# Transposing the heads of the second chunk by DMA, and holding back half of two weight matrices, in an AdaLN transformer block

## The chip, the cores and the metric

The kernel runs on one core of a Trainium2 chip. The metric is the device time of one execution in microseconds (us). Every time below is of that core. One further execution was recorded by the hardware profiler; its span runs from the first to the last instruction that the profiler saw.

## What is computed

A transformer block with adaptive layer norm: a sequence of S = 2048 rows of D = 640 values in bf16, 32 heads of 20, causal attention with a window of 256 rows, and a gated MLP of width 1536. Cut to what matters:

```python
mod = (silu(c) @ w_mod).reshape(1, 6, 1, -1)
sa, ca, ga, sb, cb, gb = mod[:, 0], ..., mod[:, 5]

h = layernorm(x) * (1 + ca) + sa
q, k, v = heads(h @ wqkv)                        # 32 heads of 20
scores = einsum('bhqd,bhkd->bhqk', q, k) * 20 ** -0.5
scores = where(0 <= i - j < 256, scores, -1e9)
x = x + ga * (merge(softmax(scores) @ v) @ wo)

h = layernorm(x) * (1 + cb) + sb
x = x + gb * ((sigmoid(h @ w_gate) * (h @ w_up)) @ w_down)
```

## The kernel before, in words

**Tiles and stages.** `build` cuts the 2048 rows into eight chunks of 256 rows (`NCH`, `CH`), numbered `a` from 0, each of two blocks of 128 rows (`bi`). All weights stay in SBUF once loaded: `wqkv`, `wo`, `wg` (w_gate), `wu` (w_up), `wd` (w_down). The weights of the modulation are needed only at the start and are loaded in the space of others: the first part in that of `wd`, others in that of `wu` and of `hh`, the MLP's hidden values. So the loads of `wu` wait until the modulation rows that used its space are computed (`extra=o1`, line 1217).

For each chunk the stages are:

- `ln1(a)` (line 833): statistics on VectorE (DVE), normalised rows on GpSimd (POOL) or DVE, then the transposed `hT`. For the first three chunks it is turned on TensorE (PE) against an identity matrix, for the others by a transposing DMA (`transp_dma`, lines 780 to 783, on SyncE's queue, SP) and then modulated (`modulate`, L790 and L791).
- `qkv(a)` (line 868): projections through `wqkv`, in pieces of 320 columns for chunk 0 and of 480 for the others. `evac` (lines 856 to 863) copies each piece from PSUM to `stg`, on ScalarE (ACT, L859) or DVE (L860); V goes to its own tiles. In `stg` a head takes 32 columns. It has four slots, each with q or k of one block of 128 rows: 128 x 1024.
- **Turning the heads.** Scores need q and k with the head's 20 values on partitions: `QT` and `KT`. Line 903 decides how a `stg` slot is turned. For chunks `a < NPQ` PE does it, in two halves of four 128x128 transposes into one PSUM tile (L911, recorded at L666, the line of the helper `mm`), and `evac` copies 512 columns out. For later chunks one transposing DMA turns the slot as a whole (line 919, recorded at L782). With PE the two halves of a slot come free to their readers one by one; with the DMA both halves come together.
- `attention(a)` (line 1074): for each half `q` of the heads five score sets (four for the heads, one for the edges of the window); for chunk 0 three. `score_set` (line 931) writes scores into the single score buffer in PSUM (PE, L667), and the exponentials are taken from it by ACT (L981). POOL masks them (L1006). Then comes a burst of 64 matmuls with V (`burst`, line 1019), which runs within a later score set, and the normalisation on DVE (`norm`, line 1044). The rows go out to DRAM and come back as `oT`, by DMA. The first score set of a chunk reads `QT` of both blocks and `KT` of its own and the previous chunk.
- `outproj(a)` (line 1113) and `mlp(a)` (line 1161): output projection, second layer norm, `h2T` by transposing DMA; then gate and up for 128 columns of FF at a time, in pairs, their product into `hh`, and the product with `wd`. Pairs from the seventh on (`f0` of 6 or more) read the second half of the columns of `wg` and `wu`.

**Loads.** `load_bulk` (line 607) splits a weight matrix by tiles of 128 rows. `wg` and `wu` are each loaded in two halves of 768 columns, and each half as a piece of three row tiles (576 KB) and one of two (384 KB): line 744 for `wg`, line 1217 for `wu`. Most of the DMAs, the transposing ones among them, go out on SP's one queue, in program order; a DMA that waits for its source holds those behind it. Each DMA also waits for the one 24 places earlier (`NDMA`), whose semaphore it takes over.

**Order.** All operations are first collected by `Prog.op`, each with a rough duration, its reads and writes, a priority and at times an earliest time (`tmin`). `Prog.schedule` (line 152) uses these to give every tile its slot. The order that runs is written out by hand, or by a search: `PRIO` (lines 341 to 464) holds a number for each operation, in the order of their making. Sorted by these numbers, the operations stand in the order of the program on each engine; the remainder of such a number after division by 5 names its engine (PE, ACT, DVE, POOL, SP). At run time nothing but these queues and the semaphores counts: `tmin` holds nothing back by itself.

Of the kernel before, what the change touches and what calls it, by code (L numbers as in the profile page):

```python
# [336 lines left out]
def c_pe(n):  # L337
# [5 lines left out]
    13, 18, 68, 1113, 43, 33, 8, 23, 53, 58, 38, 63, 48, 372, 73, 3, 96, 104, 81, 189, 199, 194, 204, 209, 219, 249,  # L343
    214, 244, 239, 234, 414, 599, 874, 574, 899, 909, 1239, 884, 904, 135, 142, 171, 177, 182, 77, 110, 115, 120,
    125, 255, 260, 265, 28, 130, 270, 290, 275, 280, 285, 295, 300, 375, 305, 322, 604, 889, 879, 1574, 914, 894,
    107, 147, 157, 92, 87, 152, 163, 168, 222, 227, 315, 350, 310, 380, 385, 340, 326, 356, 332, 391, 347, 362, 367,
    337, 401, 396, 430, 435, 446, 655, 660, 677, 480, 486, 750, 756, 415, 420, 426, 490, 495, 501, 465, 471, 650,
    682, 450, 455, 461, 520, 525, 531, 505, 577, 625, 632, 475, 510, 516, 620, 640, 646, 665, 671, 965, 981, 720,
    725, 732, 850, 865, 946, 745, 760, 767, 770, 785, 791, 547, 537, 552, 542, 442, 557, 563, 568, 612, 637, 795,
    775, 735, 855, 700, 847, 782, 742, 862, 707, 960, 970, 976, 1090, 1100, 1202, 1030, 1077, 1355, 1362, 1165,  # L350
    1170, 1191, 1277, 1205, 1291, 1375, 1382, 990, 995, 1001, 1025, 1045, 1051, 1365, 1371, 1280, 1336, 1005, 1010,
    1016, 1021, 1095, 1177, 1240, 1246, 1180, 1185, 1196, 1265, 1270, 1297, 1310, 1317, 1479, 1644, 1322, 1437,
    2114, 1494, 1894, 1499, 1862, 1902, 1922, 1947, 2142, 1385, 1522, 1529, 2854, 1467, 1507, 254, 409, 607, 952,
    957, 932, 617, 987, 1058, 1063, 1068, 1143, 1107, 1455, 1415, 1420, 1400, 1300, 1462, 1432, 1426, 1412, 1307,
    1610, 1620, 1627, 1545, 1550, 1557, 1649, 1615, 1630, 1636, 1667, 1654, 1870, 1880, 1966, 2040, 2050, 2057,
    2334, 2030, 2035, 2047, 2137, 2119, 1785, 1795, 1912, 1975, 1980, 1987, 714, 719, 917, 922, 1072, 927, 937, 942,
    1118, 1123, 1128, 1133, 1222, 1139, 1234, 1608, 1598, 1593, 1473, 1536, 580, 586, 591, 685, 691, 696, 800, 816,
    826, 806, 836, 823, 833, 813, 843, 1080, 1212, 1147, 1217, 1227, 1287, 1821, 1841, 1541, 1351, 2006, 1035, 1041,
    1086, 1150, 1156, 1161, 1250, 1326, 1391, 1341, 1256, 1333, 1398, 1348, 1263, 1500, 1512, 1517, 1562, 1662,
    1672, 1836, 1801, 1846, 1856, 2011, 2200, 2270, 2302, 2150, 2160, 2307, 2145, 2155, 2282, 2410, 2415, 2422,  # L360
    2312, 2317, 2442, 2432, 2427, 2437, 2448, 2453, 2457, 2462, 2554, 2559, 2758, 2743, 2748, 2716, 2753, 2564,
    2829, 2964, 2859, 3037, 3047, 3387, 3042, 3052, 3342, 3352, 3362, 3368, 3347, 3357, 3477, 2885, 2890, 2895,
    2900, 2905, 2765, 2770, 2775, 2790, 2880, 2916, 2942, 3085, 3090, 3115, 3120, 3125, 2910, 3095, 3100, 3105,
    3110, 3131, 3137, 3140, 3145, 3150, 3175, 3180, 3205, 3210, 3215, 3220, 3225, 3186, 3237, 3240, 3245, 3250,
    3255, 3260, 3230, 3265, 3270, 3275, 3280, 3286, 3292, 3295, 3300, 3305, 3320, 3325, 3390, 3395, 3400, 3405,
    3410, 3331, 3442, 3445, 3450, 3455, 3460, 3465, 3415, 3420, 3470, 3530, 3565, 3486, 3592, 3515, 3670, 3720,
    3727, 3730, 3745, 3750, 3757, 4119, 3765, 3805, 3830, 3872, 3660, 3665, 3825, 3877, 3884, 1715, 1790, 1867,
    1875, 1955, 1972, 2104, 1720, 1725, 1806, 1812, 2109, 2390, 2395, 2402, 2285, 2290, 2296, 2409, 2250, 2320,
    2326, 2532, 2339, 1915, 1950, 2026, 1730, 1755, 1997, 1406, 1484, 1762, 1752, 1777, 1767, 1567, 1772, 1783,
    1898, 2088, 2183, 2078, 2128, 2189, 2174, 2363, 2371, 2386, 2376, 2381, 1440, 1451, 1446, 1575, 1581, 1586,  # L370
    1675, 1701, 1681, 1736, 1696, 1740, 1826, 1816, 1830, 1851, 1886, 1960, 2016, 2021, 1533, 1713, 1708, 1603,
    1688, 1693, 1908, 2068, 1928, 2063, 2073, 2083, 2090, 2096, 2211, 2207, 2197, 2277, 2597, 2602, 2874, 2869,
    2984, 2849, 2994, 2220, 2236, 2226, 2241, 2246, 2340, 2346, 2356, 2465, 2496, 2476, 2480, 2485, 2627, 2470,
    2490, 2506, 2714, 2615, 2620, 2657, 2672, 3029, 2520, 2525, 2587, 2535, 2540, 2611, 2639, 2680, 2685, 2812,
    2816, 3034, 2650, 2665, 2787, 2795, 2875, 2937, 1659, 1489, 1992, 1937, 2002, 1932, 1747, 1942, 2123, 2133,
    2168, 2193, 2693, 2698, 2549, 2709, 3542, 2921, 3506, 3426, 3431, 2500, 2516, 2511, 2178, 2263, 2268, 2218,
    2233, 2258, 2353, 2578, 2368, 2573, 2568, 2583, 2590, 2641, 2646, 2662, 2782, 2807, 2822, 2947, 2974, 2954,
    2959, 2969, 2989, 3495, 3500, 3547, 3520, 3525, 3572, 3555, 3560, 3677, 3580, 3585, 3682, 3597, 3692, 3697,
    3702, 3687, 3707, 3713, 3718, 3777, 3862, 3784, 3869, 4158, 4153, 4143, 4021, 4136, 4175, 4300, 4310, 4315,
    4320, 4160, 4210, 4305, 4330, 4335, 4326, 4347, 4340, 4435, 4440, 4445, 4450, 4390, 4395, 4425, 4430, 4460,  # L380
    4456, 4552, 4465, 4470, 4475, 4480, 4485, 4560, 4565, 4570, 4575, 4580, 4496, 4602, 4585, 4590, 4595, 4660,
    4665, 4605, 4610, 4670, 4675, 4685, 4681, 4692, 4695, 4700, 4705, 4710, 4715, 4725, 4730, 4735, 4745, 4750,
    4721, 4767, 4770, 4780, 4830, 4835, 4840, 4805, 4810, 4815, 4820, 4825, 4846, 4857, 4850, 4915, 4920, 4927,
    5150, 5250, 5260, 5322, 5326, 5065, 5070, 5075, 5107, 5330, 5335, 5340, 5347, 5529, 2675, 2726, 2731, 2736,
    2721, 2830, 2836, 2841, 3055, 3061, 3066, 3170, 3196, 3191, 2703, 3018, 2803, 2763, 3008, 2998, 3003, 3023,
    3013, 3078, 3073, 3083, 3310, 3316, 3336, 3372, 3382, 3437, 3552, 3842, 4064, 4059, 3849, 3854, 4069, 3480,
    3511, 3601, 3606, 3491, 3610, 3641, 3616, 3735, 3741, 3796, 3760, 3925, 3932, 4200, 4205, 4227, 4239, 4075,
    4085, 4102, 4107, 4234, 4110, 4180, 4187, 3915, 3920, 3936, 4424, 3945, 3950, 4017, 4082, 4419, 3965, 3970,
    4012, 4070, 4090, 4097, 2631, 2606, 3157, 3162, 3167, 2927, 2932, 3377, 3658, 3898, 3902, 3912, 3999, 4054,
    4993, 4546, 4557, 4966, 4266, 3810, 3821, 3816, 3203, 3623, 3638, 3628, 3788, 3633, 3653, 3648, 3773, 3793,  # L390
    3803, 3893, 3940, 3956, 3961, 4002, 4007, 4352, 4357, 4362, 4369, 4384, 4374, 4379, 4389, 4910, 4930, 4937,
    4940, 4945, 4952, 4985, 5005, 5027, 5010, 5015, 5032, 5022, 5082, 5087, 5057, 5037, 5062, 5093, 5098, 5157,
    5162, 5174, 5169, 5401, 5367, 5388, 5392, 5396, 5430, 5435, 5440, 5445, 5450, 5490, 5495, 5500, 5505, 5510,
    5481, 5522, 5515, 5540, 5545, 5550, 5555, 5535, 5565, 5575, 5580, 5585, 5561, 5592, 5745, 5750, 5755, 5760,
    5825, 5775, 5785, 5790, 5850, 5855, 5831, 5867, 5875, 5880, 5885, 5895, 5900, 5860, 5890, 5905, 5930, 5965,
    5911, 5987, 5970, 5975, 5980, 5990, 5995, 6000, 6005, 6010, 6015, 6055, 6021, 6062, 6085, 6090, 6095, 6100,
    6105, 6065, 6070, 6075, 6080, 6130, 6111, 6197, 6285, 6350, 6355, 6432, 6760, 6845, 6855, 6862, 6956, 6370,
    6655, 6745, 6802, 6850, 6915, 6945, 6952, 6964, 4025, 4046, 4036, 4031, 4041, 4120, 4131, 4126, 4260, 4271,
    4281, 4400, 4406, 4411, 4173, 4193, 4198, 4148, 4293, 4168, 4248, 4253, 4258, 4278, 4288, 4298, 4500, 4531,
    4526, 4512, 4507, 4517, 4742, 4862, 5229, 5179, 5234, 4869, 5239, 4615, 4626, 4621, 4631, 4636, 4775, 4786,  # L400
    4796, 4880, 4886, 4891, 6440, 6445, 6467, 6470, 6475, 6481, 6489, 6490, 6520, 6527, 6536, 6559, 6515, 6540,
    6547, 6415, 6420, 6426, 6554, 6580, 6585, 6596, 6601, 6609, 5110, 5120, 5266, 5360, 5420, 5427, 2864, 2979,
    3537, 3887, 3907, 3577, 3837, 3857, 3978, 3983, 3987, 3992, 4219, 4224, 4493, 4538, 4762, 4756, 4521, 4955,
    4971, 4976, 4653, 4648, 4658, 4543, 4643, 4878, 4793, 4873, 4803, 4898, 4908, 4903, 5040, 5046, 5051, 5102,
# [57 lines left out]
NPQ = 2  # L462
# [810 lines left out]
```

## Time and profile before

| | |
|---|---|
| median of three runs | 328.59 us (327.43, 328.59, 805.26) |
| profiled execution, its own time | 327.7 us |
| its span | 326.0 us |
| its mean granted clock of PE | 1.00 |
| busy: PE, DVE, ACT, POOL | 318.1, 208.2, 210.6, 187.4 us |
| instructions: PE, DVE, ACT, POOL | 4877, 416, 311, 282 |
| mean DMA rate over the span | 116 GB/s |

The profiled execution took 1.7 us more than its span. A busy time is the sum of an engine's instructions, without its waits, its branches and the issuing of DMAs. The page also divides the span into 40 slices, with the busy share of each engine in tenths; PEclk there is the clock that PE was granted. Groups of instructions stand as `line engine operation output<-input shapes xcount | busy us, mean ns of one | idle us of the engine just before them, and what ended most of it`. A line of the timeline begins with start and length in us. One of the chain of waits too: it is the work that ended last, followed back step by step to what released it. PE M stands for matmuls other than scores, PE S for scores.

### The profile page before, as it was taken

How to read it: one execution, taken by the hardware profiler on the slowest of the kernel's cores; microseconds unless marked ns; L12 is line 12 of the kernel's file. 1: busy time of each engine (PE TensorE's matmuls, PEld its weight loads, DVE VectorE, ACT ScalarE, POOL GpSimd, SP SyncE). 2: the span in 40 equal slices, each digit the busy share in tenths (PEclk: the TensorE clock that was granted, in tenths of full speed). 3: DMA queues.
4: the chain of work that ended last, by engine and by line, in shares of the span. 5: the costliest groups of instructions: out<-in, count | busy, mean ns of one | idle time of the engine just before them, and what ended most of it. 6: DMA issues, size and time to landing. Idle time of an engine off the chain costs nothing.

```text
span 326.0 us, 11617 instructions
## 1 busy us (share of the span) xinstructions
PE 318.1 (98%) x4877; PEld 223.6 (69%) x4878; DVE 208.2 (64%) x416; ACT 210.6 (65%) x311; POOL 187.4 (57%) x282
## 2 busy tenths in 40 slices
PE   8999999979999999999999999999999999999996
PEld 3664644536876568765777567877786788787885
DVE  4598998559897847776576456846383666363332
ACT  1698985797875788858687878785778671021120
POOL 6119588989829795737483859564848493013000
PEclk9999999999999999999999999999999999999999
DMA  7989898999850535405804582510132131302101
GB/s 242 369 274 364 222 243 210 194 136 217 243 114 0 115 95 100 95 4 137 128 23 54 120 132 69 117 39 4 62 58 68 42 70 35 102 22 43 40 2 40
DMA packets 71694, 37.85 MB, mean 116 GB/s; under 512 B 45274, under 2 KB 70362, under 8 KB 71642
## 3 DMA queue, kind: packets, MB, share of 16 engines
q1 hardware_dynamic: 68800, 34.82, 44.6%
q10 hardware_dynamic: 2842, 2.30, 2.7%
q8 instruction: 38, 0.62, 0.8%
q14 instruction: 14, 0.11, 0.1%
HBM read 21.30 MB, written 5.25 MB: 81 GB/s over the span
## 4 chain that ended last, share of the span: by engine, by line
PE 80%; DMA 1%; ACT 1%; DVE 0%; issue 0%
PE M L666 66%; PE S L667 7%; PE M L667 6%; DMA QT<-stg 1%; ACT E L981 1%; DVE stg L860 0%; ACT V L859 0%; DVE x L1196 0%; DVE x L1130 0%
## 5 line engine op out<-in xcount | busy, mean ns | idle before, releaser
L981 ACT ACTIVATE E<-S 128x512 bf16<-128x512 f32 (+2 forms) x184 | 150.8, 879 | 49.5 <-PE S L667 46.9
L1006 POOL TENSOR_SCALAR_AFFINE_SELECT E<-E 128x512 bf16<-128x512 bf16 (+1 forms) x176 | 141.1, 830 | 68.0 <-ACT E L981 65.5
L666 PE MATMUL M<-wqkv,hT 128*128 128x480 bf16 (+1 forms) x340 | 73.4, 355 | 1.1 <-ACT hT L790 0.5
L666 PE MATMUL M<-h2T,wg 128*128 128x256 bf16 x480 | 66.1, 273 | 0.0
L666 PE MATMUL M<-h2T,wu 128*128 128x256 bf16 x480 | 66.0, 273 | 0.0
L666 PE MATMUL M<-wd,hh 128*128 128x320 bf16 (+1 forms) x396 | 59.0, 295 | 0.0
L1175 ACT ACTIVATE sig<-M 128x512 f32<-128x512 f32 x48 | 28.6, 602 | 44.0 <-PE M L666 33.8
L1177 DVE SCALAR_TENSOR_TENSOR hh<-sig,M 128x512 bf16<-128x512 f32 x48 | 32.3, 676 | 37.0 <-PE M L666 17.8
L666 PEld LDWEIGHTS M<-h2T,wu 128*128 128x128 bf16 x480 | 45.6, 98 | 7.6 <-issue 0.2
L666 PEld LDWEIGHTS M<-h2T,wg 128*128 128x128 bf16 x480 | 45.8, 98 | 7.0
L666 PEld LDWEIGHTS M<-wqkv,hT 128*128 128x128 bf16 x340 | 30.4, 98 | 28.0 <-issue 1.8
L666 PEld LDWEIGHTS M<-wd,hh 128*128 128x128 bf16 x396 | 37.0, 98 | 14.1
L667 PEld LDWEIGHTS S<-QT,KT 20*64 20x64 bf16 (+1 forms) x1856 | 20.0, 100 | 21.0 <-ACT E L981 12.6
L667 PE MATMUL S<-QT,KT 20*64 20x256 bf16 (+5 forms) x1856 | 32.3, 228 | 1.4 <-ACT E L981 1.4
L1196 DVE TENSOR_TENSOR x<-M,x 128x320 bf16<-128x320 f32 (+2 forms) x33 | 15.6, 476 | 28.2 <-PE M L666 28.0
L755 DVE BATCH_NORM_STATS2 st<-x 128x6 f32<-128x320 bf16 x64 | 28.6, 478 | 3.1 <-DMA x<-in_A_x_dram 2.6
L1048 DVE STREAM_TRANSPOSE T<-M 128x512 f32<-128x512 f32 x32 | 21.5, 696 | 10.2 <-PE S L667 7.9
L666 PE MATMUL M<-wo,oT 128*128 128x320 bf16 x160 | 25.6, 300 | 0.0
L667 PE MATMUL M<-E,V 128*32 128x128 bf16 (+1 forms) x960 | 22.8, 246 | 0.7 <-ACT V L859 0.5
L667 PEld LDWEIGHTS M<-E,V 128*32 128x32 bf16 x960 | 19.1, 97 | 5.3 <-issue 2.7
L760 POOL TENSOR_SCALAR st<-st 128x2 f32<-128x2 f32 x16 | 3.8, 238 | 32.4 <-DVE st L757 30.9
L860 DVE CAST stg<-M 128x480 bf16<-128x480 f32 (+1 forms) x24 | 14.3, 599 | 9.6 <-PE M L666 9.4
(74 smaller groups left out, 243.4 us busy)
## 6 DMA issues: line engine op xcount, KB each, us to landing
x<-in_A_x_dram SPq DMA_DIRECT2D x20, 160.0 KB
doc<-On SPq DMA_DIRECT2D x56, 40.0 KB
wd<-in_B_w_down_dram SPq DMA_DIRECT2D x4, 480.0 KB
out_dram<-x SPq DMA_DIRECT2D x11, 160.0 KB
wd<-in_w_mod_dram SPq DMA_DIRECT2D x5, 320.0 KB
wqkv<-in_A_wqkv_dram SPq DMA_DIRECT2D x4, 400.0 KB
wu<-in_w_mod_dram SPq DMA_DIRECT2D x5, 320.0 KB
oT<-doc SPq DMA_DIRECT2D x7, 192.0 KB
```

The lines of the kernel that those rows point to most:

```text
L666: return e.matmul(o, l, r, start=st, stop=sp, skip_group_check=True)
L667: return e.matmul(o, l, r, start=st, stop=sp, tile_position=tp, skip_group_check=True)
L755: A("dve", lambda e, g, bi=bi, j=j: e.bn_stats(v(bi * 12 + j * 6, 6), src[bi].ap[:, j * 320:(j + 1) * 320]), 0.48, reads=[src[bi].r()], wr ...
L760: A("pool", lambda e, g: e.tensor_scalar(v(28, n), var(), EPS, None, op0=ALU.add), 0.2, reads=[st.r(("m", bi)) for bi in range(n)], writes ...
L860: return e.tensor_copy(dst(), src())
L981: A("act", lambda e, eng: e.activation(dst(), src(), ACT.Exp, scale=SM_SCALE), c_act(n), reads=[Sp.r()], writes=[E.r(key)], prio=3, tag=f" ...
L1006: A("pool", lambda e, eng: e.affine_select(rows(dst), rows(src), pattern=[[0, 8], [sign, n]], compare_op=ALU.is_ge, fill=0.0, base=base, c ...
L1048: A("dve", lambda e, g, h=h: e.transpose(T1.ap[:, 512 * h:512 * h + 512], X[h].ap), 0.694, reads=[X[h].r()], writes=[T1.r(h)], prio=3.5, t ...
L1175: A("act", lambda e, g, pg=pg, sg=sg: e.activation(sg.ap[:], pg.ap[:], ACT.Tanh, scale=0.5), c_act(512), reads=[pg.r()], writes=[sg.r()], ...
L1177: A("dve", lambda e, g, pu=pu, sg=sg, f0=f0: e.scalar_tensor_tensor(out=hh.ap[:, f0:f0 + 2, :], in0=sg.ap[:].rearrange("p (a b) -> p a b", ...
L1196: A("dve", lambda e, g, ps=ps, bi=bi, c0=c0, n=n: e.tensor_tensor(x1[bi].ap[:, c0:c0 + n], ps.ap[:, 0:n], x1[bi].ap[:, c0:c0 + n], op=ALU. ...
```

## The change

Three things are changed.

1. `NPQ` goes from 2 to 1: q and k of chunk 1, too, are turned by transposing DMAs, one for each of the four `stg` slots.
2. The second halves of `wg` and `wu` get an earliest time of 68 us in the plan (`tmin=68.0 * h`, h being 0 or 1).
3. `PRIO` is searched anew: the list is another one throughout. It has 2105 operations in place of 2117: 8 on PE (half a slot each) and their 8 evacuations are gone, 4 DMAs are new.

```diff
-NPQ = 2
+NPQ = 1
...
     for h in range(2):
         load_bulk(wg[:, :, h * 768:h * 768 + 768], ..., R_wg[h],
-                  0.65, 0.7 + 0.2 * h, f"wg{h}", lat=0.8 + DSAFE, cuts=(3, 5))
+                  0.65, 0.7 + 0.2 * h, f"wg{h}", lat=0.8 + DSAFE, tmin=68.0 * h, cuts=(3, 5))
...
     for h in range(2):
         load_bulk(wu[:, :, h * 768:h * 768 + 768], ..., R_wu[h],
-                  0.65, 0.8 + 0.2 * h, f"wu{h}", lat=0.8 + DSAFE, extra=o1, cuts=(3, 5))
+                  0.65, 0.8 + 0.2 * h, f"wu{h}", lat=0.8 + DSAFE, tmin=68.0 * h, extra=o1, cuts=(3, 5))
```

The line of `qkv` that reads `NPQ`, unchanged:

```python
if a < NPQ or (a, key, bi) in PQ:
    for half in range(2):
        ...                        # four transposes on PE, then evac of 512 columns
else:
    transp_dma(lambda dst=dst, bi=bi: dst.ap[:, :, bi * 128:bi * 128 + 128], lambda s=s: s.ap[:], 3, 1.0,
               [s.r(i) for i in range(4)], [dst.r((bi, 0)), dst.r((bi, 1))], 1.28, f"qkt{a}")
```

Of the new `PRIO`, what the order of the program shows: on PE 4846 matmuls in place of 4878, the 32 being transposes of `stg`; on SP 54 transposing DMAs in place of 50. On ACT there are 38 instructions at L859 in place of 46, on DVE 52 at L860 in both; ACT has 2 more modulations (L790) and POOL 2 fewer (L791). One load of x and two stores of the output go out on SP's queue in place of ACT's. On SP the loads of the first rows of x stand ahead of the first load of `wqkv`. The four new transposes go out in the order K, Q, Q, (hT of chunk 2), K, (hT of chunk 2). Of `wg` only the first 576 KB stay early; the first half of `wu` follows them, and the second halves of both go out behind the transposes of q and k of chunks 2 and 3, around the first `h2T` and the first load of `wd`.

232 rows, old and new, of the table PRIO are left out of this document.

## The prediction

> **What bounds the kernel now.** I read the page first: engines' busy time and the 40 slices.
>
> ```profile
> PE 318.1 (98%) x4877; PEld 223.6 (69%) x4878; DVE 208.2 (64%) x416; ACT 210.6 (65%) x311; POOL 187.4 (57%) x282
> PE   8999999979999999999999999999999999999996
> PEclk9999999999999999999999999999999999999999
> ```
>
> TensorE (PE) is busy for 318.1 of 326.0 us, at full granted clock in every slice. So only less PE work or less PE idle can shorten the run. Where the idle lies is in the busy time by stretch (start:end, length, then busy us and instruction count of PE, PEld, DVE, ACT, POOL, the clock, the DMA share, GB/s).
>
> ```profile
> 0.00:10.00 10.00, 7.97 (x68) 3.56 (x69) 3.73 (x12) 1.49 (x2) 5.20 (x28) 1.00 0.81 264
> 30.00:40.00 10.00, 9.75 (x173) 5.82 (x172) 9.61 (x21) 8.71 (x15) 7.14 (x9) 1.00 0.90 253
> 40.00:50.00 10.00, 9.73 (x144) 4.50 (x143) 9.45 (x22) 8.39 (x14) 7.79 (x12) 1.00 0.97 240
> 60.00:70.00 10.00, 8.34 (x138) 3.98 (x137) 5.85 (x15) 9.45 (x16) 8.56 (x13) 1.00 1.09 143
> 70.00:80.00 10.00, 9.64 (x205) 5.48 (x190) 7.53 (x13) 7.46 (x13) 9.11 (x13) 1.00 0.99 198
> 80.00:323.40 243.40, 243.39 (x3811) 182.17 (x3809) 147.83 (x279) 151.54 (x215) 133.32 (x184) 1.00 0.33 73
> 323.40:326.00 2.60, 0.00 (x0) 0.00 (x0) 0.29 (x1) 0.00 (x0) 0.00 (x0) 1.00 0.23 63
> ```
>
> The span is a sum: 318.07 of PE work, 5.3 of PE idle before 80 us (2.03 in the first ten, 0.28, 0.25, 0.27, 0.47, 1.66 and 0.36 in those that follow, none in 20:30), 0.01 after it, 2.60 of tail. From 80 us on PE has no gap, so the end moves exactly as far as the work ahead of 80 us comes earlier. Next the timeline of the part that the change touches, and the chain of waits behind it.
>
> ```profile
> 36.10 0.84 PE L666 MATMUL M<-ident,stg 128*128 128x128 bf16 x12
> 38.24 0.43 PE L667 MATMUL S<-QT,KT 20*64 20x256 bf16 x24
> 41.06 0.65 PE L667 MATMUL S<-QT,KT 20*64 20x256 bf16 x24
> 41.78 1.94 ACT L981 ACTIVATE E<-S 128x512 bf16<-128x512 f32 x2 [0.55 <-PE S L667]
> 43.77 0.41 PE L667 MATMUL S<-QT,KT 20*128 20x64 bf16 x32
> ```
>
> ```profile
> 60.99 2.54 PE M L666 x13
> 65.73 4.68 DMA QT<-stg
> 74.17 0.36 PE S L667 x24
> ```
>
> 38.24 is the first score of chunk 1. From there to 74 us the scores follow each other every 2.6 to 2.8 us: one score buffer in PSUM, score, exponentials (1.94 us on ACT), next score. Between them PE does projections and other filling work. DVE (9.6 and 9.5 of 10 us at 30:50) and POOL are nearly full too. The chain also shows one transposing DMA of 4.68 us, in the stretch with the most PE idle.
>
> **The change, part by part.**
>
> *Removed.* Chunk 1's q and k heads lose 32 of the 64 PE transposes and their eight copies out of PSUM.
>
> ```profile
> L666 PE MATMUL M<-ident,stg 128*128 128x128 bf16 x64 | 5.7, 219 | 0.0
> L859 ACT ACTIVATE KT<-M 128x512 bf16<-128x512 f32 x5 | 3.2, 632 | 0.0
> L860 DVE CAST QT<-M 128x512 bf16<-128x512 f32 x4 | 2.7, 682 | 2.1 <-PE M L666 2.1
> ```
>
> PE: 5.7 / 64 = 89 ns each, 32 of them 2.85 us; by the run of twelve at 36.10 (0.84 / 12 = 70 ns) it is 2.24. Copies: eight of about 635 ns. The order of the new program shows 38 instead of 46 ACT instructions at L859 and an unchanged 52 of DVE at L860, so net all eight, 8 x 0.635 = 5.1 us, come off ACT and none off DVE (it takes over copies of `stg` instead), which is the fuller of the two here. The eight lay before 38 us, not in the score cycle, so what they are worth is at most an earlier first score.
>
> *Added.* Four transposing DMAs of 128x1024 on SP's queue.
>
> ```profile
> L782 SPq DMA_TRANSPOSE QT<-stg x12: 1231/1244/1959, 43.9 to 189.8; - x12
> 31.77 2.62 SPq L782 DMA_TRANSPOSE hT<-x  x2
> 56.87 1.23 SPq L782 DMA_TRANSPOSE KT<-stg  x1
> ```
>
> (Min, median, max ns.) SP is held 1.24 us by each, 5 us in all, or up to 8 at the maximum. From issue to landing the trace's transfer records give 3.06 us for the best of the existing ones (KT at 64.03, landed 67.0), 6.1 for the worst (56.87, landed 62.97, just behind a load of w_up). In the new order the four go out with the two hT transposes of the next chunk among them: K, Q, Q, hT, K, hT. What stands behind them on SP (wo, the gate row, x rows, w_up's first half) is held by those 5 us. In the trace of before wo went out at 34.43, the gate row at 36.57, and the output projection that uses both comes after 60 us, so this is hidden; the cover is over ten us. One more wait lies in that queue: the last gate row waits for DVE, by my walk until about 47 us (it went out at 41.70), and a part of w_up, of w_gate and a K transpose of chunk 3 stand behind it; their users come after 65 us, so I cost it at nothing with some 10 us of cover.
>
> The first score of chunk 1 needs all four. The last K transpose waits behind hT, whose source the new POOL order makes ready at about 32.3 us (hand walk from durations of before: POOL's rows up to it), so it is issued at about 32.3 + 1.31 (half of the 2.62 row) = 33.6. It lands at 36.7 with 3.06 us and at 39.7 with 6.1. DVE's row of work ahead of that score (copies of V, q and k, gate and modulation rows, 9.61 of 10 us busy in 30:40) lets PE get there at about 38.1. I take 4.1 us, the middle of the others seen (4.6, 4.1, 3.8, 3.6, 5.5): landing 37.7, just in time; 39.7 is kept as the late end.
>
> *Moved: weights.* The second halves of w_gate and w_up, 576 + 384 KB each by the table of DMA issues, went out by 57 us (the last of w_up at 56.02) and now go out at about 63 to 77, behind the heads' transposes of chunks 2 and 3. The DMA share is 0.8 to 1.1 in all stretches to 80 us, so the early ones get lighter and 60:80 heavier. MLP(0) starts at 78.0 and reaches second-half columns at 84 to 86; with 4 to 6 us a load (w_up's at 56.02 landed at 60.6) they arrive at 80 to 82. Cost 0; the cover is 2 to 6 us, and each us beyond it is a us of PE idle.
>
> *Moved: order.* The loads of x stand ahead of the first of wqkv (0.45 us later for wqkv; the first projection at 11.66 waits for the modulation rows as well): 0 to +0.45, taken at 0.2, and absorbed since DVE sets 38.1. By the counts nothing else is added: DVE 52 and 52, the modulations of hT and h2T are split anew (ACT +2, POOL -2, 0.6 us each), one load of x and two stores of the output go from ACT's queue to SP's.
>
> *Sum.* The removed 2.85 us all lie before 38.24, but the score starts at 38.1 instead of 38.24. So at first only 0.14 us is gained; some 0.5 us of projection (two 480-wide matmuls at 203 ns and a pair of x transposes) is done ahead of it, and the rest is idle. Walking the cycle on with the rows of before and the new order I get scores at 40.5, 43.0, 45.6, 49.4 and 52.0 (before 41.06, 43.77, 46.38, 49.07, 52.57), and 73.45 for the one that was at 74.10. That is 0.65 us. The walk took the 4.68 us transposition as it stands; with lighter queues ahead of it a part of the 1.66 us idle of 60:70 can go as well. I take 1.1, between 0.65 and 1.66. After that score PE has the same work in both kernels. Profiled run: 327.7 us, span 326.0 and 1.7 around it; 327.7 - 1.1 = 326.6. The runs shown have a median of 328.59 (0.9 above the profiled one) and a lowest of 327.43.
>
> **The rivals.**
>
> 1. *Forecast: a small gain*, 0 to 2 us, 325.7 to 327.7. For it: DVE and the score cycle, not PE, pace 30 to 74 us. Chance 0.53.
>
> 2. *All of the PE work is gained*: 2.85 gives 324.9, with the 1.66 of idle 323.2. For it: PE idles only 3.3 of the 70 us from 10 to 80, so work taken out there is near to being time. Against: filling work done earlier leaves PE empty later as long as the cycle is unchanged. Chance 0.20.
>
> 3. *The other side: the last K transpose of chunk 1 is late.* It decides when it lands after 38.1, so with more than 4.5 us from issue, or with hT's source later than 33 us. At 6.1 us the score runs at 39.7, 1.6 later, and 0.5 is left against before: 328.2. If the hT transpose ahead of it has such a landing too and holds it, another 2.4: 330.6. For it: 56.87 behind a bulk load, and modulation weights are still in flight at 34.5. Against: the held-back halves are no longer in these queues. Chance 0.20. The Trainium skill speaks for this side: its page "VectorE: DVE Perf Modes", sections "The three transpose paths" and "Rules for kernel authors", puts a 128x128 transpose at 390 ns on TensorE and 1309 ns by DMA, and advises TensorE where PSUM will do. Eight such tiles in a row would be 10.5 us by that figure, an estimate, and the score about 6 us late (333). This trace does not agree: DMAs of eight tiles landed 3.06 to 6.1 us after issue.
>
> 4. *The second halves of w_gate or w_up come late for MLP(0).* It decides beyond 84 us for the first. At 8 to 10 us late, which needs twice the longest landing seen, 334 to 337. Chance 0.05. For it: each load stands behind six or more transposes on one queue.
>
> Something else: 0.02.
>
> **How the numbers follow.** A measurement of this kernel can tell about 2% from no change, 6.6 us: below 321.1 or above 334.3. The point is rival 1's, 326.6. Below 321.1 would need more than both terms of rival 2: 0.03. Above 334.3: rival 4 and the end of rival 3, 0.06. Within: 0.91. The range takes rival 2 down to 323.2 and rival 3 up to 330.6; outside lie rival 4 and the ends of the others, under 2 in 10. The likeliest case's own range is 325.7 to 327.7.
>
> **What would show it.** 32 matmuls fewer at M<-ident,stg and 38 at L859 on ACT: the removal. First chunk-1 score at 38 in the timeline and its wait put down to DVE or POOL: step 2 right; put down to DMA KT<-stg: rival 3. PE busy near 315.3 with idle before 80 us up from 5.3 to 7: rival 1; idle still 5.3: rival 2. Any PE idle after 80 us with wg or wu as releaser: rival 4. What would make it wrong above all: a different pace of the score cycle between 38 and 74, since DVE and POOL have new orders there that I walked by hand.

## The result: 0.7% slower

The changed kernel takes 330.55 us (median of 11 runs) against 329.28 us (11 runs). The ratio of the two is 1.0069, with a 95% interval of 1.0044 to 1.0094: by this ratio some 2.3 us slower (the two medians differ by 1.3 us), where 1.1 us of gain was forecast. Six more timings of it gave 1.0101 (1.0064 to 1.0138). The first profiled execution of the changed kernel ran at a granted clock of 0.95, took 337.94 us, and is used neither in the ratios nor below. Two more were profiled, called profile 2 (329.25 us) and profile 3 (331.92 us, span 330.2 us).

The page of profile 2, its busy times, slices of PE and granted clock:

```profile
PE 318.3 (97%) x4846; PEld 221.7 (68%) x4846; DVE 211.6 (65%) x416; ACT 207.4 (63%) x304; POOL 187.4 (57%) x281
PE   8999999879999999999999999999999999999997
PEclk9999999979999999999999999999999999999999
```

There are 32 matmuls fewer, and PE is busy for as long as before. The ninth digit of PEclk is new: the clock was lowered for a while. The busy times by stretch of profile 2, columns as before:

```profile
30.00:40.00 10.00, 9.05 (x167) 4.76 (x166) 9.17 (x21) 6.83 (x11) 8.39 (x11) 1.00 0.80 179
40.00:50.00 10.00, 9.42 (x119) 4.22 (x118) 9.18 (x22) 7.59 (x12) 6.60 (x13) 1.00 0.99 228
60.00:70.00 10.00, 8.11 (x97) 3.75 (x80) 8.00 (x17) 7.29 (x11) 7.97 (x12) 0.85 0.81 150
70.00:80.00 10.00, 9.52 (x177) 5.00 (x176) 8.57 (x16) 6.94 (x12) 5.77 (x9) 0.98 1.09 237
80.00:324.90 244.90, 244.65 (x3840) 182.88 (x3838) 147.48 (x272) 154.52 (x221) 136.72 (x188) 1.00 0.36 77
```

The clock is 0.85 and 0.98 in 60:80, so 1.7 us of clock are missing; at half speed that is a stretch of 3.4 us. PE does only 97 matmuls in 60:70 (138 before). The timeline of profile 2 there:

```profile
65.12 0.43 PE L667 MATMUL S<-QT,KT 20*64 20x256 bf16 x24 [0.30 <-ACT E L981]
65.13 1.82 POOL L1006 TENSOR_SCALAR_AFFINE_SELECT E<-E 128x512 bf16<-128x512 bf16 x2 [0.36 <-ACT E L981]
65.79 1.24 DVE L791 TENSOR_SCALAR hT<-hT,mA 128x256 bf16<-128x256 bf16 x1
66.41 0.60 ACT L790 ACTIVATE hT<-hT,mA 128x256 bf16<-128x256 bf16 x1
67.13 3.83 PE L666 MATMUL M<-wqkv,hT 128*128 128x480 bf16 x10 [1.58 <-POOL E L1006]
70.89 0.43 PE L667 MATMUL S<-QT,KT 20*64 20x256 bf16 x24
```

After the score at 65.12 PE stands still for 1.58 us. The profile names POOL as the releaser, but what the projection of chunk 4 reads is hT, and its second tile (modulation 1, counted from 0) is modulated by DVE at 65.79. That instruction ends at 67.03, 0.1 us before PE goes on, and it took 1.24 us. The first two matmuls of a projection need modulations 0 and 1, the other three modulations 2 to 4. Modulation 2 stood on ACT behind an exponential and ended at 67.01, so it was as late as the one on DVE. In the kernel before, four modulations ran on ACT in one piece, and PE waited for the last of them:

```profile
65.82 2.07 ACT L790 ACTIVATE hT<-hT,mA 128x256 bf16<-128x256 bf16 x4
67.95 1.39 PE L666 MATMUL M<-wqkv,hT 128*128 128x480 bf16 x6 [0.45 <-ACT hT L790]
```

DVE's rows for this line, in the kernel before and in profile 3 (min, median, max ns):

```profile
L791 DVE TENSOR_SCALAR hT<-hT,mA x3: 327/333/582, 95.5 to 132.8; 128x256 bf16<-128x256 bf16 x3
```

```profile
L791 DVE TENSOR_SCALAR h2T<-h2T,scB,shB x4: 305/900/1124, 80.5 to 116.6; 128x256 bf16<-128x256 bf16 x4
L791 DVE TENSOR_SCALAR hT<-hT,mA x3: 345/505/1239, 39.9 to 67.8; 128x256 bf16<-128x256 bf16 x3
```

It takes some 0.33 us when POOL is quiet, and up to 1.24 us beside POOL's masks. Each one held by a mask ends within 0.1 us of the mask's end (67.03 and 66.95 in profile 2): DVE is held until POOL's instruction is through. In the kernel before, this tile of chunk 4's hT was modulated by ACT, and the three tiles of chunk 0's h2T that are now DVE's by POOL and ACT. The counts by engine had not shown that.

After the idle time PE runs at half clock: ten matmuls of 480 columns take 3.83 us at 67.13, where 2.2 us is usual. Profile 3 shows the other face of it:

```profile
39.26 0.43 PE L667 MATMUL S<-QT,KT 20*64 20x256 bf16 x24 [2.02 <-DMA KT<-stg]
...
67.80 1.24 DVE L791 TENSOR_SCALAR hT<-hT,mA 128x256 bf16<-128x256 bf16 x1
...
69.14 2.19 PE L666 MATMUL M<-wqkv,hT 128*128 128x480 bf16 x10 [1.58 <-POOL E L1006]
...
79.85 3.32 POOL L1006 TENSOR_SCALAR_AFFINE_SELECT E<-E 128x1024 bf16<-128x1024 bf16 x3
80.49 2.76 DVE L791 TENSOR_SCALAR h2T<-h2T,scB,shB 128x256 bf16<-128x256 bf16 x3
...
82.70 0.39 PE L666 MATMUL M<-h2T,wg 128*128 128x256 bf16 x2 [1.47 <-DVE h2T L791]
```

The same wait of 1.58 us, but the clock stays up (2.19 us). PE is then on time for MLP(0), and finds h2T not ready: its three modulations on DVE meet the masks too (2.76 us for three), and PE waits 1.47 us. In profile 3, and not in profile 2, the first score of chunk 1 also waited 2.02 us for the last K transposition. Starts of comparable work, counted from the first score of chunk 0 (16.55, 15.52, 16.15 and 16.15 us in the four timelines; `a_mod2` is an experiment below):

| from there to | before | profile 2 | profile 3 | a_mod2 |
|---|---|---|---|---|
| first score of chunk 1 | 21.69 | 21.47 | 23.11 | 21.47 |
| score just ahead of the projection of chunk 4 | 49.44 | 49.60 | 50.98 | 48.54 |
| next score | 53.21 | 55.37 | 55.11 | 51.83 |
| the score at 74.10 of before | 57.55 | 59.84 | 60.00 | 56.60 |
| end of the span | 309.45 | 311.98 | 314.05 | 308.85 |

Profile 2 is on time up to the second row, and 2.0 us further back in the row after it. Profile 3 is 1.5 us behind in the second row already, by the late K transposition; it loses 0.4 us in the row after it, and 2.2 us between the last two rows, the wait for h2T among them. So by itself the wait at chunk 4 costs little (0.4 us in profile 3), since the kernel before had smaller waits in the same place.

### The profile page after: what moved, and what is told of

Its sections match the earlier page's. It is cut to its first block, busy times and chain, and to the rows that moved or that the text cites. A ratio compares the mean times of both kernels' runs of the same rounds, so it can differ in the third digit from the quotient of the medians.

```text
span 336.2 us, 11523 instructions
## 1 busy us (share of the span) xinstructions
PE 325.2 (97%) x4846; PEld 223.9 (67%) x4846; DVE 213.4 (63%) x416; ACT 207.7 (62%) x304; POOL 187.8 (56%) x281
## 4 chain that ended last, share of the span: by engine, by line
PE 89%; DVE 3%; DMA 3%; issue 2%; ACT 2%; SPq 0%; ACTq 0%; DVEq 0%
PE M L666 74%; PE S L667 8%; PE M L667 7%; DMA wd<-in_w_mod_dram 2%; ACT E L981 1%; DMA QT<-stg 1%; DVE h2T L791 1%; DVE st L755 1%; PE S L666 0%; SPq L568 0%; DVE Tn L1055 0%; DVE T L1048 0%; ACT hT L823 0%; DVE x L775 0%; DVE stg L860 0%
## 5 line engine op out<-in xcount | busy, mean ns | idle before, releaser
L666 PE MATMUL M<-wqkv,hT 128*128 128x480 bf16 (+1 forms) x340 | 74.8, 363 | 3.4 <-POOL E L1006 1.6
L666 PE MATMUL M<-h2T,wu 128*128 128x256 bf16 x480 | 71.2, 277 | 0.2 <-DVE V L860 0.2
L666 PE MATMUL M<-h2T,wg 128*128 128x256 bf16 x480 | 69.8, 277 | 1.4 <-DVE h2T L791 1.4
L666 PE MATMUL M<-wd,hh 128*128 128x320 bf16 (+2 forms) x396 | 59.4, 302 | 0.0
L1175 ACT ACTIVATE sig<-M 128x512 f32<-128x512 f32 x48 | 28.7, 601 | 49.3 <-PE M L666 39.2
L666 PEld LDWEIGHTS M<-h2T,wg 128*128 128x128 bf16 x480 | 46.7, 99 | 9.5 <-DVE h2T L791 1.8
L666 PEld LDWEIGHTS M<-wd,hh 128*128 128x128 bf16 x396 | 37.9, 99 | 15.3
L860 DVE CAST stg<-M 128x480 bf16<-128x480 f32 (+1 forms) x29 | 17.1, 595 | 15.0 <-PE M L666 14.3
L666 PE MATMUL M<-wo,oT 128*128 128x320 bf16 x160 | 26.4, 306 | 0.0
```

Of the source, the lines that this page charges most:

```text
L666: return e.matmul(o, l, r, start=st, stop=sp, skip_group_check=True)
L860: return e.tensor_copy(dst(), src())
L1175: A("act", lambda e, g, pg=pg, sg=sg: e.activation(sg.ap[:], pg.ap[:], ACT.Tanh, scale=0.5), c_act(512), reads=[pg.r()], writes=[sg.r()], ...
```

## The experiments

Each kernel is a variant of one of the two, made by moving entries of `PRIO`; the order of all other operations is kept. In `b_npq`, `b_wts` and `b_both` line numbers are 7 higher, in `a_fill` and `a_fill2` 1 to 7. A mean clock of 0.995 of a whole execution stands for one drop: 3.4 us at half speed is 1.7 of 328 us.

### The parts in the old order: after_again, b_npq, b_wts, b_both, b_wts2

`after_again` is the execution of profile 2.

> The changed kernel as it is, looked at once more, since its first profile has a granted clock of 0.95. If the slower time is more PE idle, the idle before 100 us is 8 us or more at full clock, against 5.3 before, while PE's busy time is about 315; if it is a lower clock alone, idle is about 5 and the granted clock below 1.

PE's idle time before 80 us is 6.7 us and its busy time 318.3, and the clock dropped once: between the two cases named. `b_npq` takes the transposes off PE in the old order:

```diff
-NPQ = 2
+NPQ = 1
 SP queue:  ... last modulation weights
+KT1, QT1
 hT3 (first half)
+KT1, QT1
 hT3 (second half), wo ...
```

> The kernel before with only the heads of chunk 1 turned by DMA: the PE transposes and their copies out of PSUM are taken out of the old order, and each DMA stands right behind the last copy into its stg slot. Theory A (the transposes by DMA come late for the first score of chunk 1): 1 to 4 us slower than before, the first score of chunk 1 later than 38.2 us and waiting for a DMA. Theory B (the held-back weights cost): same or up to 2 us faster than before. Theory C (the new order costs): as B.

Measured: 1.0121 (1.0087 to 1.0156), 332.07 us. Theory A held, at the upper end of what it named (3.9 us slower):

```profile
PE S L674 <- DMA QT<-stg: 6.6, 1, 6.6
```

```profile
40.00:50.00 10.00, 7.47 (x97) 3.50 (x97) 4.16 (x10) 4.36 (x5) 3.49 (x6) 0.58 1.00 289
```

The last transposition, issued at 36.87 us behind three others and an hT, landed 5.4 us later. PE waited 6.6 us; the granted clock fell during the wait and was 0.58 in the ten us that hold its end and the work behind it.

`b_wts` holds back the weights alone, to the places they have in the new order.

```diff
 SP queue, kernel before:
-wg 2nd half (3 tiles) | ... | wu 2nd half (2) | wg 2nd half (2) | ... | wu 2nd half (3)    # by 48.4 us
 hT5
+wg 2nd half (3), h2T, h2T, wg 2nd half (2)
 wd, ..., wd
+wu 2nd half (3), wu 2nd half (2)
 doc, gbc (last gate row)
```

> The kernel before with only the second halves of w_gate and w_up held back, to the same neighbours on SP's queue as in the changed kernel. Theory B (they fill the queues between 63 and 85 us when transposes and w_down are due there): 1 to 4 us slower, with PE idle between 60 and 90 us up by as much. Theories A and C: within 0.7 us of before.

Measured: 1.0061 (1.003 to 1.0092). The idle time is where theory B had it, but not for want of the weights:

```profile
87.70 2.15 DVE L1165 TENSOR_TENSOR wd<-wd,gbc 128x640 bf16<-128x640 bf16 x4 [4.09 <-DMA gbc<-gate]
...
90.50 0.83 PE L673 MATMUL M<-h2T,wg 128*128 128x256 bf16 x6 [1.92 <-DVE hh L1184]
```

The broadcast gbc of the last gate row stood behind the two loads of w_up on SP. DVE, in order, waited 4.09 us for it with the scaling of wd, the MLP's products hh stood behind that, and PE ran out of PSUM.

> Both parts in the old order. If the parts are all of it and the new order is neutral: about 2.3 us slower than before, as the changed kernel. Theory C (the new order costs): not slower than before. If the new order mends what the parts break: clearly slower than the changed kernel, by 2 us or more.

Measured: 1.0161 (1.0124 to 1.0198), a little under the sum of the two. So each part costs in the old order, and the changed kernel, with both parts in the new one, loses less. In `b_wts2` the row goes first:

```diff
 wd
+gbc (last gate row)
 wu 2nd half (3), wu 2nd half (2)
 doc
-gbc (last gate row)
```

> The run b_wts (the kernel before with the second halves of w_gate and w_up held back) with one move on SP's queue: the broadcast of the last gate row goes out ahead of the two loads of w_up, not behind. In b_wts DVE waited 4.09 us for this row and the MLP's products hh stood behind it. If that is the cost of holding the weights back: the PE idle of 2.8 us at 88 to 92 us goes, and the kernel is within 0.6 us of before (b_wts: 0.6% slower). If the weights themselves come late: still 0.6% slower, PE waiting for w_up or w_gate.

Measured: 1.0028 (1.0011 to 1.0045). The idle time ahead of hh shrank from 2.8 to 0.65 us, and about half of the loss went; that is between the two cases named, and the other half was not traced. In the changed kernel this row does stand ahead of w_up.

### The parts taken back in the new order: a_npq2, a_wts

`a_npq2` sets NPQ to 2 again (32 transposes and eight copies back, four DMAs out); `a_wts` sends the second halves early again. The transposes were put in by hand, where the order was not searched for them.

> The changed kernel with chunk 1's heads turned on PE again: the 32 transposes and eight copies put into the new order behind the copies into stg, the four DMAs taken out. If the removal on PE is a gain in the new order (its first score of chunk 1 ran 1.25 us earlier than before): 0.5 to 2.5 us slower than the changed kernel. If the DMAs for chunk 1 are what makes the changed kernel slow: faster than it by 1 us or more.

Measured: 1.0134 (1.0105 to 1.0163), slower than the changed kernel by 0.65% against its first ratio and 0.33% against its second. The first score of chunk 1 came 23.9 us after the first of chunk 0 (21.5 in the changed one).

> The changed kernel with the second halves of w_gate and w_up sent early again, at the same neighbours on SP's queue as in the kernel before. If holding them back is what lets chunk 1's transposing DMAs land in time: those land later, the first score of chunk 1 waits for a DMA at 38 us or later (36.99 in the changed kernel), and it is 1 to 4 us slower than the changed kernel. If holding them back costs in the new order as it does in the old (0.6%): about 2 us faster.

Measured: 1.0185 (1.0149 to 1.0221), 1.2% and 0.8% slower than the changed kernel in the same way, but by another road: the first score of chunk 1 was in time (21.2). The next stretch was not:

```profile
50.97 0.43 PE L667 MATMUL S<-QT,KT 20*64 20x256 bf16 x24
51.08 0.66 DVE L860 CAST stg<-M 128x480 bf16<-128x480 f32 x1 [0.99 <-PE M L666]
51.51 1.94 ACT L981 ACTIVATE E<-S 128x1536 bf16<-128x1536 f32 x2 [1.71 <-PE S L667]
52.44 1.98 PE L666 MATMUL M<-wqkv,hT 128*128 128x480 bf16 x9 [1.04 <-DMA QT<-stg]
```

On SP's queue the x rows and the heads of chunk 2 stood behind the loads. So neither part taken back by hand wins the loss back. Whether both are worth having in an order searched for them was not shown; what makes this one lose is something else in it.

### The wait at chunk 4 and the clock: a_fill, a_mod, a_mod2, a_fill2, a_h2t, after_rounds, b_mod

`a_fill` leaves the wait and keeps PE at work in it:

```diff
             if a == 4 and bi == 0 and lo == 0:
+                def dummy(e, g, ps=ps):
+                    for k in range(7):
+                        ins = e.matmul(ps.ap[:, 0:480], ident[:], wqkv[:, 0, 0:480], start=True, stop=True, skip_group_check=True)
+                    return ins
+                A("pe", dummy, ..., writes=[ps.r()], hold=[ps])
             pe_chain(ps, wid, pairs, ...)
```

> The changed kernel with seven extra 128x480 matmuls on PE just ahead of the first projection of chunk 4, at 65.5 us, where PE is idle for 1.58 us; they write into the PSUM tile that this projection then overwrites, so the result is as before. The wait itself stays. Theory G (the idle stretch makes the granted clock drop to one half for 3.41 us, and this costs): the clock is 1.00 throughout, the ten 480-column matmuls at 67.1 take 2.2 us in place of 3.83, and the kernel is about 1.6 us faster than the changed one. Theory W (only the waits count): no change, or slower by what the extra matmuls push back.

Measured: 1.0066 (1.0041 to 1.0091): no faster than the changed kernel, though no execution of six had a drop of the clock. Its timeline:

```profile
67.00 1.59 PE L892 MATMUL M<-wqkv,ident 128*128 128x480 bf16 x7
68.65 2.19 PE L667 MATMUL M<-wqkv,hT 128*128 128x480 bf16 x10
70.77 0.43 PE L668 MATMUL S<-QT,KT 20*64 20x256 bf16 x24
```

```profile
80.01 2.76 DVE L792 TENSOR_SCALAR h2T<-h2T,scB,shB 128x256 bf16<-128x256 bf16 x3
...
82.22 0.39 PE L667 MATMUL M<-h2T,wg 128*128 128x256 bf16 x2 [1.48 <-DVE h2T L792]
```

From the score ahead (66.64) to the next it takes 4.13 us in place of 5.77 in profile 2: the 1.64 us of the clock are saved there, as theory G said. They are given back at 82 us, as in profile 3. (In this trace, too, the first score of chunk 1 waited 2.0 us for K.) `a_mod` takes the wait itself away:

```diff
 POOL, from 63.6 us:
 hT4 modulation 0
+hT4 modulation 1
 masks ...
 ACT, from 64.9 us:
 hT4 modulations 3, 4
+hT4 modulation 2
 exponential
-hT4 modulation 2
 DVE:
-hT4 modulation 1
```

> The changed kernel with two modulations of chunk 4's hT moved: the one that stood on DVE beside POOL's masks (1.24 us long there) goes to POOL ahead of those masks, and the last one on ACT goes ahead of an exponential. PE's wait of 1.58 us before the first projection of chunk 4 should go down to 0.5 us or less. Theory G: no drop of the clock, 2 us or more faster than the changed kernel, about as before or a little faster. Theory W: faster by the wait alone, 0.5 to 1.1 us.

Measured: 0.9997 (0.997 to 1.0025), 327.83 us: the whole loss is gone. PE no longer stops between the score and the projection:

```profile
65.57 0.43 PE L667 MATMUL S<-QT,KT 20*64 20x256 bf16 x24 [0.30 <-ACT E L981]
65.93 2.49 PE L666 MATMUL M<-wqkv,hT 128*128 128x480 bf16 x10
68.86 0.43 PE L667 MATMUL S<-QT,KT 20*64 20x256 bf16 x24 [0.43 <-ACT E L981]
```

It moved two modulations: modulation 1 away from DVE and its collision, and modulation 2 on ACT ahead of an exponential. No run moves only one of them. With modulation 1 alone in time, four of the ten matmuls could have gone ahead in profile 2, some 0.8 us (an estimate: they start 0.2 us apart), and the other six would still have waited for ACT until 67.01. So without the collision alone about half of the 1.58 us would go, and the rest takes ACT's order as well. In `a_mod` itself the ten take 2.49 us in place of 2.19: the last six start as ACT's last modulation ends.

Here h2T met a mask only with its third modulation, and PE did not wait for it. `a_mod2` puts those three on POOL as well; `a_fill2` has the extra matmuls and h2T on POOL; `a_h2t` has h2T on POOL alone.

```diff
-h2T(0) modulations 1, 0, 3 on DVE
+h2T(0) modulations 1, 0, 3 on POOL
```

> The changed kernel with the modulations of chunk 4's hT as in the run a_mod and the three modulations of chunk 0's h2T on POOL in place of DVE, as in the kernel before. If DVE beside POOL's masks is the whole of the loss: mean clock 1.00, no PE wait for h2T, 0.5 to 1.1 us faster than before (what was forecast for the change). If a_mod was all that there is to mend: same as before within 0.5 us.

> The changed kernel with the seven extra matmuls of a_fill and with the three modulations of chunk 0's h2T on POOL. In a_fill the 1.64 us that the higher clock saved at 66 to 71 us were given back at 81 us, where DVE's modulations of h2T took 2.76 us in place of 1.72 beside POOL's masks and PE waited 1.48 us. If that is so, they stay saved here: 1 to 1.7 us faster than the changed kernel and than a_fill, about 0.3% slower than before. If the clock is worth nothing: as the changed kernel, 0.7% slower than before.

> The changed kernel with only the three modulations of chunk 0's h2T on POOL in place of DVE; it differs from a_fill2 by the seven extra matmuls alone, and from a_mod2 by the modulations of chunk 4's hT alone. Theory G (the drop of the clock costs by itself): mean clock 0.995 in most runs, about 0.7% slower than before, and 0.2 to 0.5% slower than a_fill2. If the clock costs nothing: as a_fill2 or faster.

> The changed kernel itself on the same chip, to set beside a_h2t and, by its profile, beside the first two looks: 0.4 to 0.9% slower than before, mean clock 0.995 in most runs; PE idle of about 1.6 us in one piece before the first projection of chunk 4 in this profile too.

Measured: `a_mod2` 1.0003 (0.9979 to 1.0027), `a_fill2` 1.0049 (1.0023 to 1.0076), `a_h2t` 1.0026 (1.0004 to 1.0049), `after_rounds` (profile 3) 1.0101 (1.0064 to 1.0138). `a_fill2` lost more than the 0.3% expected, with a drop of the clock in three of its 12 executions, and `after_rounds` a little more than the 0.9%, with a drop in three of six. `a_h2t` still has the wait at chunk 4:

```profile
66.25 1.24 DVE L791 TENSOR_SCALAR hT<-hT,mA 128x256 bf16<-128x256 bf16 x1
...
67.59 2.19 PE L666 MATMUL M<-wqkv,hT 128*128 128x480 bf16 x10 [1.58 <-POOL E L1006]
```

Theory G in the form "the drop of the clock is the whole cost" does not hold: `a_fill` had no drop and lost as much as the changed kernel. `a_h2t` does not decide it, since it had a drop in only two of 12 executions, after a wait of the same length. The changed kernel had one in eight of the 10 executions counted the first time and in three of six the second, and those without were not clearly faster. In `a_mod` a drop does go with a longer time: the two executions that had one took 330.6 and 331.3 us, the other ten 326.7 to 329.6.

What fits all of these: the wait at chunk 4 is followed by either the half clock (1.6 us) or the wait for h2T (1.5 us), and either costs the same. This is argued from single traces, profile 2 for the one, profile 3, `a_npq2` and `a_wts` for the other (waits of 1.6 us at chunk 4 and 1.5 us for h2T in all three). Where the drop came in executions without a trace is not known; in the trace of `a_wts` it came after the wait for h2T. With both waits taken out the loss is gone (`a_mod2`, and `a_mod`, in whose trace h2T was in time); with the second alone taken out most of it is (`a_h2t`). None of them reaches the gain that was expected.

`b_mod` puts the one suspect into the kernel before:

```diff
-hT4 modulation 1 on ACT
+hT4 modulation 1 on DVE, after two statistics of the same stretch
```

> The kernel before with one thing taken from the new order: the second modulation of chunk 4's hT runs on DVE, beside POOL's masks, in place of ACT. If DVE's modulation being held by POOL's masks is the cause: it takes about 1.2 us in place of 0.4, PE waits 1.2 us or more in one piece before the first projection of chunk 4 (0.24 us before), the granted clock falls to a mean of 0.995 in a part of the runs, and the kernel is 0.7 to 2.5 us slower than before. If the cause lies elsewhere in the new order: within 0.5 us of before.

Measured: 1.0013 (0.9987 to 1.0038): no clear loss. The modulation began only 0.25 us before the end of the mask and took 0.33 us, PE's wait was one of 1.07 us in place of three smaller ones, and all ten matmuls then ran in one piece:

```profile
67.88 0.33 DVE L791 TENSOR_SCALAR hT<-hT,mA 128x256 bf16<-128x256 bf16 x1
...
68.31 2.19 PE L666 MATMUL M<-wqkv,hT 128*128 128x480 bf16 x10 [1.07 <-POOL E L1006]
```

So it did not make the collision that it was to make. That one such collision is enough by itself to slow the old order was not shown.

## Why the prediction was wrong, point by point

**The removal.** The count was right (32 matmuls and eight instructions at L859 fewer). Its size was not:

```profile
L666 PE MATMUL M<-ident,stg 128*128 128x128 bf16 x32 | 2.9, 219 | 0.0
```

The row halves, from 5.7 to 2.9 us, but PE's busy time in the traces of the new order at full clock is 317.5 (profile 3), 317.1 (`a_mod` and `a_mod2`) and 316.1 us (`a_h2t`) against 318.1: 0.6 to 2.0 less, not 2.85. A part may be this: the busy time of a group holds the end of its last matmul, which can overlap what follows. Without it the run of twelve at 36.10 gives about 56 ns each ((0.84 - 0.22) / 11, with 0.22 us for one alone), 1.8 us for 32. The remainder was not traced.

**The first score of chunk 1.** Forecast 0.14 us earlier and set by DVE; measured 0.22 earlier in profile 2. The time was near, the reason was not: its weight load (PEld) waited 0.24 us there for the K transposition, not for DVE. The landing, forecast at 37.7, was at 36.9 in profile 2, and at 39.2 in profile 3, 4.9 us after its issue. The late landing is rival 3, and it happened in two of seven traces of kernels that keep this stretch of the new order (profile 3 and `a_fill`), at 1.4 to 1.6 us each. What makes a transposition take 3.3 us in one execution and 4.9 in another stays open. (The hT in that queue is chunk 3's, not the next chunk's or chunk 2's, as the prediction and the section on the change had it; nothing hangs on that.)

**The walk to 74 us.** It held for 25 us: the scores at 40.5, 43.0 and 45.6 were at 39.5, 42.1 and 44.7 in profile 2, with a start 1.0 us earlier. It failed at one place, the projection of chunk 4, where it let 1.66 us of idle time shrink; it became a wait of 1.58 us in one piece with a sequel of as much again. In the table the 74.10 mark should have been 0.65 earlier and was 2.29 later. With the modulations set back it came 0.95 earlier in the trace of `a_mod2`, so the walk's direction holds there; the medians of whole executions show nothing of this gain.

**The step that failed** is "Moved: order", costed at 0: "the modulations of hT and h2T are split anew (ACT +2, POOL -2, 0.6 us each)". I counted instructions for each engine and did not look which ones had changed engine, where in its engine's order each now stands, nor what POOL does at that time; the walk took their durations from before. In its place the runs showed a wait of 1.58 us ahead of the projection of chunk 4, for a modulation held to 1.24 us on DVE and one late on ACT, and behind it 1.6 us of half clock or 1.5 us of waiting for h2T. That is worth 0.7% (`a_mod` against the changed kernel), the whole of the loss. How it divides between DVE and ACT stays open. The sentence "DVE and POOL have new orders there that I walked by hand" named the place, but the prediction gave it no chance of its own.

**The weights.** Cost 0 was right for the new order: no PE wait for wg or wu after 80 us in any trace of it, and sending them early again by hand costs 0.8 to 1.2%. What stands behind them on the queue, not the weights, was the danger (`b_wts`).

**The rivals.** Rival 1's mechanism, that the score cycle and not PE's work sets the pace, is what the mended kernels point to: from 10 to 80 us PE idles 4.4 us in `a_mod` and 4.0 in `a_mod2` against 3.3 before, so most of the 1.0 us by which their busy time is less comes back as idle time, and the time of the whole stays within 0.3%. By the sign that the prediction named, idle before 80 us, it is not clear: 6.5 and 5.5 us lie between the 7 of rival 1 and the 5.3 of rival 2, since the idle time of the first ten us differs too (2.1 and 1.6 us, 2.0 before). A gain of 0.9% or more, as rival 2 had it, is excluded for these kernels, and rival 1's own 0.34% is at the edge of their intervals or beyond. No rival had the collision or the clock. The Trainium skill has both. Its page "SBUF — State Buffer", section "Who interferes with whom", says that VectorE in its two-port modes and GpSimd lock each other out of a shared port for a whole instruction; the rows above agree (0.33 us alone, 1.24 us beside a mask), though no trace shows the mode. Its page "TensorE: Matmul & The Clock Gate", section "What's actually happening", describes a clock at one half after an idle window of about 3.4 us; the length of the drop agrees, but the idle time ahead of it here was 1.58 us, and the same wait was followed by it in profile 2 and not in profile 3.

## What to carry to other kernels

When an order is searched anew, list for each short operation on the way to the bound engine which engine had it before and has it now, what stands ahead of it there, and, for one on DVE, what POOL does at that time; equal counts hide it. A wait that is removed may uncover the next one: in `a_fill` the saving at 66 us came back as a wait at 82 us. Behind a held-back load look for the small transfers that its queue carries next, since an in-order engine that waits for one of them holds everything behind it.

## What the runs showed of the hardware

A modulation of 128x256 in bf16 on DVE took 0.30 to 0.35 us alone and up to 1.24 us when it met a mask of POOL. DVE's instruction ended within 0.1 us of the mask's, so it waited and was not merely slowed. A PE idle time of 1.58 us (profile 2) was followed by a granted clock of one half for 3.4 us, and idle times of 1.58 and 2.02 us in profile 3 and of 1.58 us in `a_h2t` were not. In `b_npq`, with a wait of 6.6 us, the clock was 0.91 and 0.58 in two stretches of ten, which is 10.2 us at half speed. Of 83 executions of the kernel before, one had such a drop. A transposing DMA of 128x1024 landed 3.3 us after its issue in one execution and 4.9 us in another of the same program.
